# Second layer of a fused attention and feed-forward kernel by seven block products, in a phase of its own

## The chip, the cores and the metric

One core of one Trainium2 chip runs the whole program. The metric is the device time of one execution in microseconds (us); the figure before is the median of three runs. Engines are named as the profile names them: PE (matrix engine; PEld is its weight load), DVE (VectorE), ACT (ScalarE), POOL (GpSimd), SP (SyncE, which here only issues DMAs).

## The reference, cut to what matters

```python
kv  = einsum('bhsd,bhse->bhde', k, v)          # 8 batches, 8 heads, 576 positions, 64 wide
out = einsum('bhsd,bhde->bhse', q, kv)
x   = out / sqrt(mean(out * out, -1) + 1e-6) * g_norm      # to [4608 tokens, 512]
h   = x @ w_in                                  # 512 -> 2048
y   = gelu(h) @ w_out                           # 2048 -> 512, gelu with erf
```

All arrays are fp32.

## The kernel before, in words

The 4608 tokens are worked on in nine chunks (0 to 8) of 512. For a chunk, linear attention and its normalisation give `o` (four tiles of 128 features by 512 tokens), the first layer gives 16 tiles `h` of 128 by 512, GELU makes them into `g`, and the second layer adds 16 products into four PSUM banks `acc0` to `acc3`, one for 128 tokens. While one chunk is in the two layers, the attention of the next is prepared: `project` and `squares` (ACT squares and copies), `reduce`, `fold`, `rsqrt` (nine small DVE instructions), `scale` (a DVE transposition that spreads the factors, through the single buffer `sq`, and a multiplication). `sum_kv` and `split_kv` make the key-value matrices two chunks ahead.

PE multiplies in a fast form that keeps fewer mantissa bits than fp32. So each operand is split in two parts, a high one (a cast by ACT) and a low one (a subtraction by DVE or POOL, "low" below), and a product takes three matmuls: high by high, high by low, low by high. `split_q`, `high_block`/`low_block` and `gelu`/`rest` make such pairs.

From chunk 2 on (`PLAIN = 2`) the first layer multiplies 2 by 2 blocks with seven products instead of eight (Winograd's form of Strassen's scheme): pairs of h tiles, j = 0 to 7, in `layer1_pair`. Sums of weight blocks are made once, in chunk 1 (`combine`, `high_sums`, `low_sums`), and are written to DRAM as `products`; sums of activation blocks (T1 to T4, `add_blocks`) are made for each chunk. Per pair there are 7 x 6 matmuls of 256 columns (line 454); DVE adds the products up in PSUM (line 446). The products come back from DRAM through a ring of four tiles of 512 KB (`load_products`), a fetch being issued when the matmuls of the tile that it replaces are done. The second layer is plain: 16 x 12 matmuls of 512 columns per chunk (line 573), with `w_out`'s two parts lying in SBUF throughout. PE takes turns: a pair of the first layer, then the two second-layer products of the pair before.

The schedule is manual: on each engine the instructions stand in the order in which the code is written, and semaphores are put in from the data's dependencies. The DMAs stand in one queue, SP's, and one that waits holds those behind it.

Of the kernel before, what the change touches and what calls it, by code (L numbers as in the profile page):

```python
# [16 lines left out]
P = 128  # L17
# [5 lines left out]
PLAIN = 2  # L23
HALF = CH // 2
RING = 4
# [11 lines left out]
def linear_attn_rms_gelu_ffn(  # L37
# [31 lines left out]
    ps_acc = ctx.enter_context(tc.tile_pool(name="ps_acc", bufs=1, space=PSUM))  # L69
    ps_h = ctx.enter_context(tc.tile_pool(name="ps_h", bufs=2, space=PSUM))  # L70
    ps_a = ctx.enter_context(tc.tile_pool(name="ps_a", bufs=2, space=PSUM))
    dram = ctx.enter_context(tc.tile_pool(name="dram", bufs=1, space=bass.MemoryType.DRAM))

    HI, LO = slice(0, DM), slice(DM, 2 * DM)
    kv_h = [const.tile([P, NP, P], F32R, name=f"kv_h{s}") for s in range(2)]
# [7 lines left out]
    AWAY, ROOM = 48, 64  # L83

    def block_tile(name, dtype):
        ring = name in [f"w_in{i}" for i in range(RING)]
        return const.tile([P, 2 * DM + (ROOM if ring else 0)], dtype, name=name)
# [20 lines left out]
    def load_tails(b):  # L108

        tails = const.tile([P, 2 * DM], F32, name="w_in4")[:TAIL].rearrange("p (a n) -> p a n", a=NP)  # L110
        nc.sync.dma_start(out=tails[:, 2:], in_=kv_tail[b, :, 2:])
        for p in (2, 3):
            kv_in[b, p].append((tails[:, p, :P], tails[:, p, P:]))

    def load_kv(b, p):
# [4 lines left out]
        elif b == PLAIN + 1 and p > 1:  # L120
            main = const.tile([P, 2 * DM], F32, name=f"w_in{8 + p}")
# [26 lines left out]
    def sum_kv(b, pairs, ps=None):  # L148

        first = 0 if ps is not None else pairs[0]  # L150
        if ps is None:
            ps = kv_ps[b, first] = ps_a.tile([P, 512], F32, name="ps_a")
# [21 lines left out]
    class Attn:  # L174
# [34 lines left out]
        def project(self, p):  # L209
            qh, ql = self.qs.pop(p)  # L210
            ps = ps_a.tile([P, 512], F32, name="ps_a")
# [34 lines left out]
        def fold(self, n=NP):  # L246
            ps = ps_a.tile([P, 512], F32, name="ps_a")[:, :n * NB]
            nc.tensor.matmul(
                out=ps.rearrange("p (g b) -> p g b", g=n), lhsT=fold, rhs=self.part[:, :n, :],
# [35 lines left out]
        def scale(self, p):  # L285
# [3 lines left out]
            nc.vector.tensor_tensor(out=o, in0=o, in1=bc, op=ALU.mult)  # L289
# [27 lines left out]
        def add_blocks(self, k):  # L317
# [12 lines left out]
            nc.vector.tensor_tensor(out=t, in0=a, in1=b, op=op)  # L330
            self.sums[k] = t

        def high_block(self, n):

            x = piece_tile(self.c, n)
# [14 lines left out]
    NT2 = NPR * NF // 4  # L350
# [8 lines left out]
    def piece_tile(c, n):  # L359
        k = (["x2", "x3"] + [f"w_in{i}" for i in range(5, 10)],  # L360
             ["x0", "x1", "x4", "x5"] + [f"w_in{i}" for i in range(10, 13)])[c % 2][n]
        return const.tile([P, 2, 2, HALF], F32R, name=k)

    products = [dram.tile([P, 2 * DM], F32, name=f"products{t}") for t in range(NT2)]

    def product_out(j, k, src):

        n = NPR * j + k
        to = products[n // 2][:, n % 2 * DM:(n % 2 + 1) * DM]
        nc.sync.dma_start(out=to.rearrange("p (a n) -> p a n", a=2), in_=src.bitcast(F32))  # L370
# [3 lines left out]
    def combine(j, second):  # L374

        if not second:
            whole.clear()
            for a in range(2):
# [4 lines left out]
                if a == 0:  # L383
                    product_out(j, 0, t[:, :, :HALF])
                    product_out(j, 4, t[:, :, HALF:])
                else:
                    product_out(j, 3, t[:, :, HALF:])
# [24 lines left out]
    def low_sums():  # L412
        for (j, second), (s, t) in halved.items():
# [3 lines left out]
            for a, k in enumerate((6, 5) if second else (1, 2)):  # L417
                product_out(j, k, t[:, a])
        halved.clear()

    ring = {}

    def load_products(t):
        if t < (NCH - PLAIN) * NT2:
            reused(t % RING, F32R)
            to, src = kept[t % RING], products[t % NT2]
            first = [not n % NPR for n in (2 * t, 2 * t + 1)]
            for a in range(2):
                at = a * DM + (a * ROOM if first[a] else AWAY)
                ring[2 * t + a] = to[:, at:at + DM]  # L430
            if any(first):
# [632 lines left out]
```

## Time and profile before

| | |
|---|---|
| median of the runs | 823.49 us (822.92 to 824.34, three runs) |
| profiled execution: span from first to last instruction | 821.7 us; the profile gives no other time for it |
| PE, PEld busy | 816.0 us (99%), 721.8 us (88%) |
| DVE, ACT, POOL busy | 496.1 us (60%), 313.8 us (38%), 65.7 us (8%) |
| DMA | 174.99 MB, mean 213 GB/s |
| plain second layer, line 573 | 46% of the chain that ended last |
| first layer by blocks, line 454 | 33% of it |

The chain that ended last is followed back from the last instruction, at each step to what released it. PE is in it nearly all the time: what PE does, one thing after the other, is the kernel's time, and what the other engines do counts where PE waits for it.

### The profile page before, as it was taken

To read this page: it belongs to the slowest core of one execution; us is meant where nothing else is said; L and a number is where in the kernel's file an instruction comes from. 1 tells how busy PE (TensorE), PEld (TensorE's weight loads), DVE (VectorE), ACT (ScalarE), POOL (GpSimd) and SP (SyncE) were. 2 spreads that over 40 slices of the span, in tenths; PEclk is the share of its full clock that TensorE was granted. 3 is DMA by queue.
4 is the path that set the end of the run, shared out by engine and by line. 5 is a ranking of instruction groups with operands and counts; after the bars stand their busy time and mean duration, and the time that the engine had idled before them with its cause. 6 is when DMAs were issued, how large, how long until landed. Compare 5 with 4: busy or idle time off the path is not lost.

```text
span 821.7 us, 13904 instructions
## 1 busy us (share of the span) xinstructions
PE 816.0 (99%) x5390; PEld 721.8 (88%) x5390; DVE 496.1 (60%) x980; ACT 313.8 (38%) x578; POOL 65.7 (8%) x69
## 2 busy tenths in 40 slices
PE   9999999999999999999999999999999999999998
PEld 7688888887999999999989999999899999999997
DVE  3999847678446745575457554674477456754443
ACT  2788544344432343232432353143423442323221
POOL 1000020102010100010100101010001000100000
PEclk9999999999999999999999999999999999999999
DMA  9981337787594569556855678456555665556551
GB/s 348 406 346 52 116 99 259 244 270 262 166 354 146 179 226 351 160 179 202 310 197 179 206 248 296 150 179 225 197 180 181 205 231 175 183 168 243 177 171 52
DMA packets 69670, 174.99 MB, mean 213 GB/s; under 512 B 7396, under 2 KB 16356, under 8 KB 69604
## 3 DMA queue, kind: packets, MB, share of 16 engines
q1 hardware_dynamic: 69600, 174.09, 61.4%
q8 instruction: 43, 0.70, 0.3%
q14 instruction: 23, 0.19, 0.1%
q10 hardware_dynamic: 4, 0.00, 0.0%
HBM read 149.95 MB, written 24.12 MB: 212 GB/s over the span
## 4 chain that ended last, share of the span: by engine, by line
PE 94%; DMA 2%; DVE 2%; issue 1%; SPq 0%; ACT 0%; DVEq 0%; ACTq 0%
PE acc L573 46%; PE ps_h L454 33%; PE ps_h L547 8%; PE ps_a L218 3%; PE ps_a L158 2%; PE ps_h L539 1%; DMA w_in<-kv_tail 1%; DMA out<-z 1%; PE ps_h L658 1%; PE acc L692 0%; DMA q<-qT 0%; DVE w_in L414 0%; DVE w L398 0%; DMA products<-x 0%; DVE gl L565 0%
## 5 line engine op out<-in xcount | busy, mean ns | idle before, releaser
L573 PE MATMUL acc<-w_out,gh 128*128 128x512 f32 x700 | 217.0, 391 | 0.0
L454 PE MATMUL ps_h<-w_in,w_in 128*128 128x256 f32 x1392 | 166.9, 276 | 0.0
L454 PEld LDWEIGHTS ps_h<-w_in,w_in 128*128 128x128 f32 x1392 | 161.9, 188 | 0.0
L573 PE MATMUL acc<-w_out,w_in 128*128 128x512 f32 x672 | 159.6, 392 | 0.0
L573 PEld LDWEIGHTS acc<-w_out,gh 128*128 128x128 f32 x700 | 129.2, 188 | 25.4
L573 PEld LDWEIGHTS acc<-w_out,w_in 128*128 128x128 f32 x672 | 123.9, 188 | 24.8
L573 PE MATMUL acc<-w_out,gl 128*128 128x512 f32 x350 | 136.4, 390 | 0.1
L559 ACT ACTIVATE gh<-ps_h 128x512 fp32r<-128x512 f32 x88 | 52.6, 597 | 202.3 <-DVE ps_h L446 146.5
L454 PEld LDWEIGHTS ps_h<-x,w_in 128*128 128x128 f32 x960 | 119.0, 189 | 4.4
L454 PE MATMUL ps_h<-x,w_in 128*128 128x256 f32 x960 | 119.8, 278 | 0.0
L464 DVE COPY w_in<-ps_h 128x256 f32<-128x256 f32 x56 | 23.8, 425 | 130.6 <-PE ps_h L454 130.6
L559 ACT ACTIVATE w_in<-ps_h 128x512 fp32r<-128x512 f32 x56 | 33.5, 598 | 178.1 <-DVE ps_h L446 178.1
L446 DVE TENSOR_TENSOR ps_h<-ps_h,w_in 128x256 f32<-128x256 f32 x168 | 72.6, 432 | 43.5 <-PE ps_h L454 39.6
L446 DVE TENSOR_TENSOR w_in<-ps_h,w_in 128x256 f32<-128x256 f32 x168 | 71.3, 424 | 42.4 <-PE ps_h L454 40.5
L547 PE MATMUL ps_h<-x,w_in 128*128 128x512 f32 x360 | 86.8, 390 | 0.0
L560 ACT ACTIVATE ps_h<-ps_h 128x512 f32<-128x512 f32 x144 | 85.5, 594 | 0.0
L565 DVE TENSOR_TENSOR gl<-ps_h,gh 128x512 fp32r<-128x512 f32 x88 | 60.4, 687 | 41.5 <-ACT ps_h L560 37.3
L547 PEld LDWEIGHTS ps_h<-x,w_in 128*128 128x128 f32 x360 | 67.4, 188 | 13.9 <-POOL x L306 0.2
L573 PEld LDWEIGHTS acc<-w_out,gl 128*128 128x128 f32 x350 | 65.7, 188 | 14.5 <-DVE gl L565 0.5
L565 DVE TENSOR_TENSOR w_in<-ps_h,w_in 128x512 fp32r<-128x512 f32 x56 | 38.4, 687 | 17.0 <-ACT ps_h L560 17.0
L206 POOL TENSOR_TENSOR ql<-q,qh 128x512 fp32r<-128x512 f32 x16 | 21.3, 1329 | 211.1 <-ACT qh L205 153.2
L341 POOL TENSOR_TENSOR w_in<-o,w_in 128x512 fp32r<-128x512 f32 x13 | 16.9, 1322 | 204.0 <-ACT w_in L336 204.0
(153 smaller groups left out, 641.8 us busy)
## 6 DMA issues: line engine op xcount, KB each, us to landing
w_in<-products SPq DMA_DIRECT2D x140, 512.0 KB, 4.6
w_in<-products SPq DMA_DIRECT2D x112, 256.0 KB, 4.9
products<-w_in SPq DMA_DIRECT2D x40, 256.0 KB, 3.4
w_in<-w_in SPq DMA_DIRECT2D x16, 512.0 KB, 10.2
kv_main<-kv_main SPq DMA_DIRECT2D x16, 512.0 KB, 7.7
w_out<-w_out SPq DMA_DIRECT2D x16, 512.0 KB, 10.2
q<-qT SPq DMA_DIRECT2D x15, 512.0 KB, 5.9
out<-w SPq DMA_DIRECT2D x18, 256.0 KB, 2.1
```

The costliest lines, as they stand in the source:

```text
L158: nc.tensor.matmul(out=ps[r, n * D:(n + 1) * D], lhsT=k[:, r], rhs=v[:, r], start=(j == 0), stop=(j == NJ),)
L206: eng.tensor_tensor(out=ql, in0=q, in1=qh.bitcast(F32), op=ALU.subtract)
L218: nc.tensor.matmul(out=ps[:, a:e], lhsT=w, rhs=x[:, a:e], start=(m == 0), stop=(m == 2))
L341: eng.tensor_tensor(out=x[:, 1], in0=self.block(OPERANDS[n]), in1=x[:, 0].bitcast(F32), op=ALU.subtract,)
L446: add = lambda out, x, y: nc.vector.tensor_tensor(out=out, in0=x, in1=y, op=ALU.add)
L454: nc.tensor.matmul(out=out, lhsT=y, rhs=x[:, z, kb], start=first and kb + i == 0, stop=kb == 1 and i == 2, skip_group_check=True,)
L464: nc.vector.tensor_copy(out=p1, in_=a[:, left])
L547: nc.tensor.matmul(out=h, lhsT=parts["in", i][:, w][:, p * P:(p + 1) * P], rhs=at.x[p][:, x], start=(m + p == 0), stop=(m == 2 and p == NP ...
L559: nc.scalar.activation(out=gh, in_=h, func=AF.Gelu)
L560: nc.scalar.activation(out=h, in_=h, func=AF.Gelu)
L565: nc.vector.tensor_tensor(out=gl, in0=h, in1=gh.bitcast(F32), op=ALU.subtract)
L573: nc.tensor.matmul(out=ps, lhsT=x[:, ts], rhs=parts["out", i][:, w], start=(i == 0 and m == 0), stop=(m == 2 and (i == NF - 1 or (i, t) == ...
```

## The change

From chunk 3 on (`FAST = 3`) a chunk goes in two phases. In the first phase the pairs of the first layer follow each other without second-layer work between; a pair is cut into a first part (products 0 to 3) and a second part (products 4 to 6), and the second part of pair j stands behind the first part of pair j + 1. Attention work stands between the parts (`within_layer1`). GELU is applied once and its result kept in fp32 (`blocks`), not split at once.

In the second phase the second layer too goes by seven block products (`class Fast`): blocks of 256 tokens by 256 features, four groups n of four h tiles for each product k, in the order of `TICKS`. A tick (k, n) is 12 matmuls of 256 columns. `ready` makes the two parts of its activation operand (ACT cast, DVE low), four ticks ahead; `combine` makes the sums and differences of activation blocks in place, on POOL for product 6 and 2 in groups 0 to 2, else on DVE; `after` adds up products and stores. `within_layer2` prepares the next chunk's first-layer operands: T1 to T4 on POOL, lows in turn on DVE and POOL. The multiplication in `scale` moves to POOL too.

`w_out`'s block sums are made in chunk 2: `sum_out` on POOL, `split_out` on ACT and DVE, written out by DMAs on ACT's queue (`send`); blocks that need no sum are written in chunk 1 on SP's queue (`raw_out`). The ring grows to six tiles and is fed from one list of fetches (`queue`) for both layers; eleven of the tiles stay in SBUF (`RESIDENT`). PSUM banks get fixed names. In chunks 0 to 2 the order on PE is as before; the last chunk ends with the second phase instead of `finish`.

```diff
-RING = 4
+FAST = 3
+RING = (0, 1, 2, 3, 10, 11)
...
-        def scale(self, p):
+        def scale(self, p, eng=nc.vector):
             bc = work.tile([P, CH], F32, name="sq")
             self.spread(p, bc)
             o = self.o[p]
-            nc.vector.tensor_tensor(out=o, in0=o, in1=bc, op=ALU.mult)
+            eng.tensor_tensor(out=o, in0=o, in1=bc, op=ALU.mult)
...
+    ORDER = (0, 2, 4, 6, 1, 3, 5)
+    GROUPS = NF // 4
+    TICKS = [(0, 0), (0, 1), (0, 2), (2, 0), (2, 1), (0, 3), (2, 2), (2, 3)]
+    TICKS += [(k, n) for k in ORDER[2:] for n in range(GROUPS)]
...
+    def second_part(at, j, blocks):
+
+        a, b, u, v = pairs_open.pop(j)
+        product(at, j, 4, a[:, left])
+        product(at, j, 5, a[:, right])
+        add(a[:, right], a[:, right], u[:, right])
+        product(at, j, 6, b[:, right])
+        add(v[:, left], b[:, right], u[:, left])
+        add(b, b, v)
+        if j % 2 == 0:
+            blocks[j // 2] = [take() for _ in range(2)]
+        for (name, t), ps in zip(blocks[j // 2], (a, b)):
+            nc.scalar.activation(
+                out=grid(t)[:, :, j % 2], in_=ps.rearrange("p (a n) -> p a n", a=2), func=AF.Gelu
+            )
...
+        def ready(self, i):
+
+            if i >= len(self.ticks):
+                return
+            k, n = self.ticks[i]
+            op = self.ops[i] = take(F32R)
+            src = self.source(k, n)
+            hi, lo = (op[1].rearrange("p (z k n) -> p z k n", z=2, k=2)[:, z] for z in range(2))
+            nc.scalar.copy(out=hi, in_=src)
+            nc.vector.tensor_tensor(out=lo, in0=src, in1=hi.bitcast(F32), op=ALU.subtract)
...
+    def sum_out(j):
+
+        eng = nc.gpsimd
+        (name, whole), (of, s) = take(), take()
+        for n in range(2):
+            w = parts["out", 2 * j + n].bitcast(F32)
+            add(whole[:, n * DM:(n + 1) * DM], w[:, HI], w[:, LO], eng=eng)
...
+    def within_layer1(c, j):
...
+                nxt.project(j, bank("a0"))
+                nxt.squares(j)
+                if j < 2:
+                    nxt.split_q(2 + j)
+            if j == NP:
+                ps = bank("a0")
+                nxt.inv = nxt.rsqrt(nxt.fold(ps))
...
+            if j == 5:
+                sum_kv(c + 2, (2, 3), kv_ps[c + 2, 0])
+                split_kv(c + 2, range(NP))
+        if aft:
+            if j == 1:
+                aft.load(0)
+            if j in (4, 5):
+                aft.split_q(j - 4)
+        if nxt and j in (5, 6):
+            nxt.scale(2 * j - 9, nc.gpsimd)
...
+            if i == 0:
+                for k in ("T3", "T1", "T2", "T4"):
+                    attn[c + 1].add_blocks(k, nc.gpsimd)
+            if i % step == step - 1 and i // step < NPR:
+                n = i // step
+                next_piece(c, n, nc.gpsimd if n % 2 else nc.vector)
...
+    for c in range(FAST, NCH):
+        at = attn[c]
+        blocks = {}
+        layer = Fast(c, blocks)
+        for j, second in parts_of_layer1():
...
+            if (j, second) == (NJ2 - 1, False):
+                free.extend(names.pop((c, n)) for n in range(4))
+                for i in (3, 4):
+                    layer.ready(i)
+            if second and j % 2:
+                last = j == NJ2 - 1
+                layer.combine(6, j // 2, nc.vector if last else nc.gpsimd)
+                layer.ready(TICKS.index((0, j // 2)))
+                layer.combine(2, j // 2, nc.vector if last else nc.gpsimd)
+        free.extend(names.pop((c, n)) for n in range(4, NPR))
+        for i in range(len(layer.ticks)):
+            if i + layer.AHEAD > TICKS.index((0, GROUPS - 1)):
+                layer.ready(i + layer.AHEAD)
+            if 5 <= i < 5 + GROUPS:
+                layer.combine(3, i - 5)
+            if 9 <= i < 9 + GROUPS:
+                layer.combine(1, i - 9)
+            layer.matmuls(i)
+            layer.after(i)
+            within_layer2(c, layer, i)
```

How this moves instructions, at three places of chunk 5. Names are those of the tiles with the number of the buffer; numbers behind are partitions by elements. First PE, before: a pair of the first layer (line 454; `ps_h` is its PSUM bank, the second name is the ring's tile) and the first of the second-layer products behind it (line 573).

```order
L454 MATMUL ps_h<-x_7247,w_in_1483 128x256 x6
L454 MATMUL ps_h<-w_in_7249,w_in_1492 128x256 x6
L454 MATMUL ps_h<-w_in_7307,w_in_1492 128x256 x6
L454 MATMUL ps_h<-w_in_7212,w_in_2050 128x256 x6
L454 MATMUL ps_h<-w_in_7214,w_in_2050 128x256 x6
L454 MATMUL ps_h<-w_in_7210,w_in_2052 128x256 x6
L573 MATMUL acc_6773<-w_out_1138,gh 128x512 x2
L573 MATMUL acc_6773<-w_out_1138,gl 128x512
```

PE now, at the change of phase: the second parts of pairs 6 and 7 (line 523), then ticks 0 to 5 (line 1140).

```order
L523 MATMUL h_5980<-w_out_5327,w_in_2070 128x256 x6
L523 MATMUL h_5980<-w_out_5380,w_in_2070 128x256 x6
L523 MATMUL h_5981<-w_out_5437,x_3243 128x256 x6
L523 MATMUL acc_6075<-w_out_5327,w_in_2072 128x256 x6
L523 MATMUL acc_6075<-w_out_5380,w_in_2072 128x256 x6
L523 MATMUL acc_6076<-w_out_5437,x_3243 128x256 x6
L1140 MATMUL acc_6175<-w_in_2198,x_5727 128x256 x12
L1140 MATMUL acc_6175<-w_in_2200,w_out_5899 128x256 x12
L1140 MATMUL acc_6175<-w_in_1471,w_out_6071 128x256 x12
L1140 MATMUL acc_6233<-w_in_1480,w_out_6111 128x256 x12
L1140 MATMUL acc_6233<-w_in_2070,w_in_6114 128x256 x12
L1140 MATMUL acc_6175<-w_in_3402,w_out_6171 128x256 x12
```

The 512-column matmuls between the pairs are gone; the second layer's operands are needed only behind the last pair, and its weights now come through the ring (`w_in_2198`, `w_in_2200`, ...). Second, DVE, before: kv halves, scaling, one pair of the first layer and its lows (line 565).

```order
L170 TENSOR_TENSOR kv_l_77<-ps_a,kv_h_75 64x4x64 x2
L293 STREAM_TRANSPOSE sq<-y 128x512
L289 TENSOR_TENSOR o<-o,sq 128x512
L464 COPY w_in_2181<-ps_h 128x256
L446 TENSOR_TENSOR w_in_2181<-ps_h,w_in_2181 128x256 x2
L446 TENSOR_TENSOR ps_h<-ps_h,w_in_2181 128x256
L446 TENSOR_TENSOR w_in_2181<-ps_h,w_in_2181 128x256
L446 TENSOR_TENSOR ps_h<-ps_h,w_in_2181 128x256 x2
L565 TENSOR_TENSOR w_in_2234<-ps_h,w_in_2234 128x512
L565 TENSOR_TENSOR w_in_2238<-ps_h,w_in_2238 128x512
```

DVE now: the end of pair 6, the last spreading of factors, the end of pair 7, then combinations (line 1107), lows of ticks (line 1118) and a low for the next chunk (line 354).

```order
L514 TENSOR_TENSOR h_5981<-h_5981,gl 128x512
L307 STREAM_TRANSPOSE sq<-y 128x512
L514 TENSOR_TENSOR acc_6075<-acc_6075,gh 128x256
L514 TENSOR_TENSOR gl<-acc_6076,gh 128x256
L514 TENSOR_TENSOR acc_6076<-acc_6076,gl 128x512
L1107 TENSOR_TENSOR w_out_6139<-x_6140,w_out_6139 128x512
L1118 TENSOR_TENSOR w_out_6171<-w_out_6139,w_out_6171 128x512
L1107 TENSOR_TENSOR w_out_6139<-w_out_6139 128x512
L1118 TENSOR_TENSOR w_out_6209<-w_in_5958,w_out_6209 128x512
L354 TENSOR_TENSOR w_out_6227<-o,w_out_6227 128x512
L1118 TENSOR_TENSOR w_out_6230<-w_out_6139,w_out_6230 128x512
```

The multiplications of `scale` have left DVE, and behind the last pair stands a row of instructions that read and write SBUF only. Third, POOL, before: all that it has in a chunk, splits of q (line 206) and two lows (line 341).

```order
L206 TENSOR_TENSOR ql<-q,qh 128x512
L206 TENSOR_TENSOR w_in_5109<-q,w_in_5109 128x512
L206 TENSOR_TENSOR ql<-q,qh 128x512
L341 TENSOR_TENSOR w_in_5562<-o,w_in_5562 128x512
L341 TENSOR_TENSOR w_in_5564<-o,w_in_5564 128x512
L206 TENSOR_TENSOR w_in_5663<-q,w_in_5663 128x512
```

POOL now, from pair 4 to the start of the second phase: splits of q (line 217), scaling (line 303), combinations (line 1107), T3, T1, T2, T4 (line 344).

```order
L217 TENSOR_TENSOR ql<-q,qh 128x512
L303 TENSOR_TENSOR o<-o,sq 128x512
L217 TENSOR_TENSOR w_in_6064<-q,w_in_6064 128x512
L303 TENSOR_TENSOR o<-o,sq 128x512
L1107 TENSOR_TENSOR w_in_5958<-w_in_5959,w_in_5958 128x512
L1107 TENSOR_TENSOR w_in_5958<-w_in_5958 128x512
L303 TENSOR_TENSOR o<-o,sq 128x512 x2
L344 TENSOR_TENSOR z<-o 128x512
L344 TENSOR_TENSOR o<-o 128x2x256
L344 TENSOR_TENSOR w<-z,o 128x512
L344 TENSOR_TENSOR z<-o,w 128x512
```

Twelve instructions now stand behind each other on POOL where two splits and two lows stood, and DVE's queue at that place waits for POOL's multiplications through the buffer `sq`.

423 lines of the change are left out of this document (332 added, 91 removed).

## The prediction

> **What bounds the kernel now.** First the page: the engines, and the chain of work that ended last.
> ```profile
> span 821.7 us, 13904 instructions
> PE 816.0 (99%) x5390; PEld 721.8 (88%) x5390; DVE 496.1 (60%) x980; ACT 313.8 (38%) x578; POOL 65.7 (8%) x69
> PE 94%; DMA 2%; DVE 2%; issue 1%; SPq 0%; ACT 0%; DVEq 0%; ACTq 0%
> ```
> TensorE (PE) is busy 99% and is 94% of the chain. Next, that chain in order of time through chunk 3 (start, length, what).
> ```profile
> 295.66 4.79 PE ps_h L454 x42
> 300.45 0.68 PE ps_a L218 x6
> ...
> 333.98 0.17 PE ps_a L248 x2
> 334.15 2.48 PE ps_a L158 x80
> ...
> 342.30 4.80 PE ps_h L454 x42
> 347.09 5.46 PE acc L573 x24
> ...
> 383.34 4.79 PE ps_h L454 x42
> ```
> One chunk is 383.34 - 295.66 = 87.7 us and PE never waits in it: eight times a pair of the first layer (4.8) and two blocks of the second (5.46), and 5.6 of projections, key-value sums and fold. A matmul of 256 columns takes 4.795/42 = 0.1142 us, one of 512 takes 5.46/24 = 0.2275. Then the stretches (busy us of PE, PEld, DVE, ACT, POOL; clock; DMA share; GB/s): a saturated load at the start, chunk 1, and a steady piece.
> ```profile
> 30.00:40.00 10.00, 10.00 (x47) 8.38 (x47) 9.00 (x17) 8.86 (x17) 0.00 (x0) 1.00 1.02 408
> 100.00:190.00 90.00, 89.91 (x473) 74.39 (x472) 63.16 (x114) 37.20 (x72) 13.47 (x10) 1.00 0.61 209
> 370.00:460.00 90.00, 90.00 (x644) 81.78 (x643) 52.58 (x107) 31.57 (x59) 7.72 (x6) 1.00 0.66 222
> ```
> In the steady piece VectorE (DVE) has 37 of 90 us free, GpSimd (POOL) nearly all, and the DMA engines move 222 GB/s where they have moved 408. The clock is 1.00.
>
> **Term 1, PE: minus 31.9.** Per chunk the plain second layer is 8 x 5.46 = 43.7 us. The block form is 28 ticks (7 products x 4 groups) of 12 matmuls of 256 columns: 336 x 0.1142 = 38.4, one tick 1.37. No row has these operands. Half of a 512-column matmul would make it 38.2 and the L454 rows, same shape and same reloading of the stationary side, 38.4; I take L454. Six chunks (3 to 8) save 5.3 each: 31.9. That gives 821.7 - 31.9 = 789.8 us of span, if nothing else moves.
>
> **Term 2, who prepares the operands: plus 24.** A tick needs its activations split into a high half (ACT) and a low half (DVE); 28 lows replace 16, ten adds of 512 ("combinations") come to DVE and six to POOL, and POOL takes over the scaling, the sums T1 to T4 and three lows: 21 instructions of POOL per chunk, six before. In the second phase itself DVE has some 42 instructions of 0.61 against 38.4 us: it fits. The tight place is the end of the first phase, where the normalisation of the next chunk, the last pairs and the first operands of the second phase stand behind each other in DVE's queue. The costs are read from a stretch of chunk 2 (DVE in order of time: start, length, what, idle before).
> ```profile
> 242.94 0.42 DVE L464 COPY w_in<-ps_h 128x256 f32<-128x256 f32 x1 [3.81 <-PE ps_h L454]
> 243.40 0.42 DVE L446 TENSOR_TENSOR w_in<-ps_h,w_in 128x256 f32<-128x256 f32 x1
> ...
> 246.80 0.90 DVE L446 TENSOR_TENSOR ps_h<-ps_h,w_in 128x256 f32<-128x256 f32 x2
> 247.61 0.68 DVE L565 TENSOR_TENSOR gl<-ps_h,gh 128x512 fp32r<-128x512 f32 x1
> 248.85 0.69 DVE L565 TENSOR_TENSOR gl<-ps_h,gh 128x512 fp32r<-128x512 f32 x1 [0.56 <-ACT ps_h L560]
> 249.46 0.21 DVE L263 TENSOR_SCALAR m<-ps_a 128x64 f32<-128x64 f32 x1
> ...
> 251.64 0.41 DVE L170 TENSOR_TENSOR kv_l<-ps_a,kv_h 64x256 fp32r<-64x256 f32 x1
> 252.48 0.43 DVE L170 TENSOR_TENSOR kv_l<-ps_a,kv_h 64x256 fp32r<-64x256 f32 x1 [0.43 <-ACT kv_h L169]
> 252.94 0.71 DVE L293 STREAM_TRANSPOSE sq<-y 128x512 f32<-128x512 f32 x1
> 253.75 0.69 DVE L289 TENSOR_TENSOR o<-o,sq 128x512 f32<-128x512 f32 x1
> ```
> Starts tell the price in a queue: 0.46 for 256 columns with a dependency, 0.61 for 512 (248.85 to 249.46), 2.2 for the inverse root (to 251.64), 1.3 for the two kv halves with their hand-over to ACT, 0.73 for a transposition.
>
> Take chunks 3 to 5, from the end of PE's second part of pair 4 to the first matmul of tick 6 that reads a low half. PE has there: fold 0.17, first parts 6 and 7 (24 matmuls, 2.74 each), second parts 5, 6, 7 (18 matmuls, 2.06 each), half of the 2.48 of kv sums, six ticks 8.2, and 0.23: 21.5 us. DVE has: the tail of pair 4 1.1, inverse root 2.2, first parts 2 x 1.34, second parts 3 x 1.5, four transpositions 2.9, kv 1.3 and half a us until ACT comes to it, five lows and two combinations 4.3, the GELU's hand-over 0.55: 20.05. So 1.45 us is left, before any meeting with POOL. POOL runs eleven or twelve instructions of 1.29 in those 21 us, and this is what a meeting costs (first POOL, then DVE, chunk 1; then a pair of groups by shape, mean ns after the bar).
> ```profile
> 184.94 1.29 POOL L341 TENSOR_TENSOR x<-o,x 128x512 fp32r<-128x512 f32 x1 [28.38 <-PE acc L573]
> 186.19 1.47 POOL L206 TENSOR_TENSOR ql<-q,qh 128x512 fp32r<-128x512 f32 x1
> 184.99 1.52 DVE L398 TENSOR_TENSOR w<-z,w 128x256 f32<-128x256 f32 x1
> 186.43 1.78 DVE L414 TENSOR_TENSOR w_in<-w,w_in 128x512 fp32r<-128x512 f32 x1
> 219.39 1.29 POOL L206 TENSOR_TENSOR ql<-q,qh 128x512 fp32r<-128x512 f32 x1 [21.19 <-PE ps_h L454]
> 220.55 0.42 DVE L446 TENSOR_TENSOR w_in<-ps_h,w_in 128x256 f32<-128x256 f32 x1
> L341 DVE TENSOR_TENSOR x<-o,x 128x512 fp32r<-128x512 f32 x13 | 12.7, 974 | 0.0
> L341 DVE TENSOR_TENSOR w_in<-z,w_in 128x512 fp32r<-128x512 f32 x11 | 7.5, 686 | 0.5 <-ACT w_in L336 0.2
> ```
> With both inputs in SBUF, the DVE instruction under a POOL instruction took 1.78 instead of 0.68 and the small one 1.52 instead of 0.42: 1.1 us each, in turn with POOL. With one input in PSUM (220.55) it took its usual 0.42. The Trainium skill ("SBUF — State Buffer", section "Who interferes with whom") says that a DVE instruction with two SBUF inputs and a GpSimd one that reads SBUF lock each other out of a shared port, the loser fully blocked; the 1.78 agrees, and by that rule every meeting costs its full price, which is the second rival below.
>
> Eight such meetings are due in the stretch: the inverse root, the five lows, the two combinations (lines 1118 and 1107 of the changed kernel, opposite POOL's q split, scaling, combinations and T sums). A meeting costs between 0.3 (974 - 686 ns, the mean of a group that met POOL now and then) and 1.1. The early four fall at random within 1.29, half of it 0.65; the late ones stand face to face, nearer 1.1, unless POOL is through. I take 0.75. Stall before tick 6: 8 x 0.75 - 1.45 = 4.55. Up to tick 16 DVE has two instructions per tick (1.22 of 1.37), so it gains little, and two more of POOL's lows come: 0.8. Chunks 3 to 5: 5.3 each. Chunk 6 has no kv work (DVE 1.8 less, PE 1.24 less): 4.8. Chunk 7 has no q split either, six meetings: 6 x 0.75 - 2.0 + 0.8 = 3.3. Chunk 8 prepares nothing: 0. Sum 24. With 0.3 a meeting the same sum is 3.4, with 1.1 it is 40.8.
>
> **Term 3, chunk 2: plus 2.** Two lows more per pair on DVE (1.2 us) and 5.2 us of POOL (two sums of 512, four of 256) make w_out's sums. What DVE had to spare at the pairs' starts:
> ```profile
> 266.31 0.42 DVE L464 COPY w_in<-ps_h 128x256 f32<-128x256 f32 x1 [0.78 <-PE ps_h L454]
> 276.57 0.43 DVE L464 COPY w_in<-ps_h 128x256 f32<-128x256 f32 x1 [0.19 <-PE ps_h L454]
> ```
> Two of eight pairs run over, by 0.4 and 1.0, with some meetings more; 0 if the waits inside a pair absorb it, 4 if not.
>
> **Term 4, DMA and queues: 0.** A fast chunk fetches 45 tiles of 0.524 MB, with 4.7 MB of q, kv and output 28.3 MB: 343 GB/s over 82.4 us, under 408. Six tiles in the ring give a fetch five tiles' time, at least 6.9 us:
> ```profile
> w_in<-products SPq DMA_DIRECT2D x140, 512.0 KB, 4.6
> ```
> Against 4.6 from issue to landing some 2.5 us are to spare. On SP's queue the q load waits for POOL's split of the chunk before and holds the fetches behind it by about as much (0 to 0.5 per chunk). Chunk 1's 18 more DMAs hide under its DMA share of 0.61, the four per pair on ACT's queue under an ACT that is busy a third; if that cover is gone, kv tails or GELUs come late, 1 us at most. The end is as before, one add and one DMA.
>
> Sum: 789.8 + 24 + 2 = 815.8 of span. The median of the runs, 823.49, lies 1.8 above the profiled span, so 817.6.
>
> **Rivals.** (a) The lock is cheap, 0.3 a meeting, and DVE keeps pace: for it the mean of 974; against it that POOL's work quadruples. 789.8 + 3.4 + 0 to 2 + 1.8 = 795 to 797. (b) Slower than before: every meeting at its full price, in this one place, between first and second phase. The sum grows by 47 us per us of price (40.8 - 3.4 over 0.8); the saving is gone at 0.88, and at 1.1 it is 789.8 + 40.8 + 4 + 1.8 = 836. For it 186.43, where two queues stood face to face; against it that POOL must have an instruction ready each time. (c) The fetches become the bound, against the 408. The second phase alone moves 21 tiles, q, kv and output, 13.9 MB in 38.4 us, 362 GB/s; were only 323 to be had, the chunk would be 87.7 as before and the change worth nothing from this alone: 823. The Trainium skill ("DMA: Bandwidth & Descriptors", section "Specifications") gives about 358 GB/s per core for HBM; by that the second phase would last 38.8, 0.4 more per chunk, 820 in all; the trace's 408 speaks against it.
>
> **Chances.** Forecast (price 0.6 to 0.84): 0.40, 810 to 822. (a), below 0.6: 0.25. (b), above 0.88: 0.27. (c): 0.08. About 0.2% (1.6 us) can be told from no change. Faster: the forecast nearly whole, (a), a little of (c): 0.62. Same 0.10, slower 0.28. The likeliest one's range is 810 to 822; for 8 in 10 both rivals are cut half through: 797 to 831.
>
> **What would show it.** PE busy about 783 with 25 us of idle, nearly all in chunks 3 to 7 around the change of phase, released by DVE lows of line 1118; none in chunk 8, whose 28 ticks take 38.4. DVE's two-SBUF instructions mean 0.8 to 1.0 us there, the 512-column add on PSUM (line 514) 0.69. Wrong in the steps: ticks longer than 1.37 (term 1); PE waiting for the ring's DMAs (term 4); stalls without any POOL beside them (term 2's count of DVE's work).

## The result and the profile after

The changed kernel takes 843.88 us (842.56 to 846.76), the kernel before, on the same chip, 823.54: ratio 1.0255, 95% interval 1.0235 to 1.0274. Forecast were 817.6 and a range of 797 to 831. First the page of the profiled execution.

```profile
span 841.8 us, 16154 instructions
PE 807.5 (96%) x6248; PEld 751.7 (89%) x6248; DVE 613.7 (73%) x1063; ACT 354.9 (42%) x654; POOL 267.8 (32%) x198
PE 74%; DVE 18%; DMA 4%; ACT 2%; issue 1%; POOL 0%; SPq 0%; ACTq 0%; DVEq 0%
```

PE was busy 816.0 us before and is busy 807.5 now: 8.5 less, where 33 less were forecast (783). Span less busy time is 34.3 us, 28.6 more than before, where 26 more were forecast. So most of the miss is on the busy side; 6.5 of it is waiting all the same, because PE counts as busy while a stopped stream drains and refills (by the starts below, its waits grew by 35.1 us, its idle time by 28.6). Next, who ended PE's waits (engine, line, waited for: us, times, longest).

```profile
PE acc L1140 <- DVE w_out L1118: 12.8, 9, 1.7
PE h L523 <- DVE w_in L514: 7.0, 5, 3.0
PE acc L523 <- DVE gl L514: 4.0, 4, 1.3
PE acc L682 <- DVE gl L674: 1.8, 1, 1.8
PE acc L523 <- DMA w_in<-products_in: 1.1, 1, 1.1
```

The first row and the third are the change of phase, as forecast; the second is chunk 2. The chain that ended last shows one change of phase, in chunk 4 (start, length, what).

```profile
437.54 0.44 DVE gl L514
...
451.14 2.76 DVE w_out L1118 x2
...
457.95 1.26 DVE w_out L1107
459.21 1.70 DVE w_out L1118
460.93 1.66 DVE w_out L1107
462.58 1.68 DVE w_out L1118
464.31 14.08 PE acc L1140 x118
478.39 5.65 PE a L1140 x48
```

From 437.5 to 464.3 DVE carries the chain, with 1.9 us of ACT in it, then PE. How long the matmuls take where PE waits for nobody is to be read in chunk 8, in the same chain:

```profile
774.52 4.93 PE acc L523 x42
...
798.42 22.64 PE acc L1140 x192
821.06 5.62 PE a L1140 x48
```

No stall, but four ticks take 5.62 us, 1.405 each, where 1.37 was forecast, and 42 matmuls of the first layer, which keeps its products, take 4.93, where 42 took 4.79 before. The granted clock is 1.00 in both profiles. Matmuls of one shape have become slower.

To put a figure on that I took, from the traces, the distance from each matmul's start to the next one's. Undisturbed it is 0.1133 us for 256 columns and 0.2268 for 512. What a distance has above that counts as "rate", or as "waits" if the distance is more than about 13% over. Sums in us, without the 24 matmuls of 512 columns in the first 28 us, which are alike in all:

```
kernel                  first layer   ticks   512 columns   waits
                        (rate)        (rate)  (rate)
before                      2.0         -         1.7         2.5
after                       9.5        8.4        3.0        37.6
e1_before_pad48             8.6         -         3.5         2.5
e2_pad64                    6.5       10.0        0.4        39.3
e3_pad64_offset48           6.3        3.5        0.5        43.2
e4_sums_on_vector           6.5        3.6        0.6        48.9
e5_before_no_zero          10.5         -         1.1         3.0
e6_zero_back                6.8        3.7        0.6        43.0
e7_prepare_late             7.2        4.5        0.6        57.3
e8_chunk2_q_later           6.4        3.5        0.5        38.8
e9_before_all16            10.6         -         1.7         2.2
e10_prepare_early           6.8        3.4        0.5        16.4
e11_in_offset16             7.3        3.4        0.6        37.3
e12_early_and_offset16      8.5        3.4        0.5        17.2
```

Not all of the last column is waiting for an operand. The granted clock is 1.00 throughout in most of these profiles, but in six it falls to 0.50 behind a stall, for 3.4 us at a time: once in e2, e7 and e12, twice in e6 and e10, five times in e4. Each time costs some 1.7 us, most of which is counted in the column: 8.5 in e4.

The change takes 6 x (192 x 0.2268 - 336 x 0.1133) = 32.9 us of PE work away, its rates give 17.1 back (20.9 against 3.8 with small rests) and its waits 35.1: +19.3, against 20.1 between the spans.

### The profile page after: what moved, and what is told of

Its sections match the earlier page's. It is cut to its first block, busy times and chain, and to the rows that moved or that the text cites. A ratio compares the mean times of both kernels' runs of the same rounds, so it can differ in the third digit from the quotient of the medians.

```text
span 841.8 us, 16154 instructions
## 1 busy us (share of the span) xinstructions
PE 807.5 (96%) x6248; PEld 751.7 (89%) x6248; DVE 613.7 (73%) x1063; ACT 354.9 (42%) x654; POOL 267.8 (32%) x198
## 4 chain that ended last, share of the span: by engine, by line
PE 74%; DVE 18%; DMA 4%; ACT 2%; issue 1%; POOL 0%; SPq 0%; ACTq 0%; DVEq 0%
PE acc L1140 15%; PE acc L523 13%; PE acc L682 12%; PE h L523 11%; PE h L655 10%; PE a L1140 8%; DVE w_out L1118 4%; PE a L230 3%; DMA w_in<-products_in 2%; DVE acc L514 2%; DVE sq L307 2%; DVE w_out L1107 1%; PE a L169 1%; DVE gl L514 1%; DMA kv_main<-kv_main 1%
## 5 line engine op out<-in xcount | busy, mean ns | idle before, releaser
L1140 PE MATMUL acc<-w_in,w_out 128*128 128x256 f32 x900 | 114.0, 281 | 12.8 <-DVE w_out L1118 12.8
L523 PE MATMUL acc<-w_out,w_in 128*128 128x256 f32 x930 | 119.5, 281 | 3.0 <-DVE gl L514 2.8
L1140 PEld LDWEIGHTS acc<-w_in,w_out 128*128 128x128 f32 x900 | 108.9, 189 | 14.7 <-DVE w_out L1118 14.7
L682 PE MATMUL acc<-w_out,gh 128*128 128x512 f32 x312 | 97.5, 394 | 0.0
L655 PE MATMUL h<-x,w_in 128*128 128x512 f32 x360 | 87.9, 393 | 0.0
L655 PEld LDWEIGHTS h<-x,w_in 128*128 128x128 f32 x360 | 67.5, 188 | 14.9
L523 PE MATMUL h<-w_out,w_in 128*128 128x256 f32 x558 | 71.9, 281 | 0.0
L682 PEld LDWEIGHTS acc<-w_out,gh 128*128 128x128 f32 x312 | 58.0, 188 | 12.3
L523 PEld LDWEIGHTS h<-w_out,w_in 128*128 128x128 f32 x558 | 68.2, 188 | 0.1
L682 PE MATMUL acc<-w_out,gl 128*128 128x512 f32 x156 | 61.3, 393 | 1.8 <-DVE gl L674 1.8
```

The costliest lines, as they stand in the source:

```text
L523: nc.tensor.matmul(out=out, lhsT=y, rhs=x[:, z, kb], start=first and kb + i == 0, stop=kb == 1 and i == 2, skip_group_check=True,)
L655: nc.tensor.matmul(out=h, lhsT=parts["in", i][:, w][:, p * P:(p + 1) * P], rhs=at.x[p][:, x], start=(m + p == 0), stop=(m == 2 and p == NP ...
L682: nc.tensor.matmul(out=ps, lhsT=x[:, ts], rhs=parts["out", i][:, w], start=(i == 0 and m == 0), stop=(m == 2 and (i == NF - 1 or (i, t) == ...
L1140: nc.tensor.matmul(out=ps[:, a * HALF:(a + 1) * HALF], lhsT=x[:, at], rhs=y, start=(k in (0, 2, 1) and n + p + a + m == 0), stop=(n == GRO ...
```

## Experiments

Each is timed against the kernel before on the same chip; e1 to e4, e5 to e8 and e9 to e12 are on three chips, where the kernel before takes 823.1, 823.5 and 823.2. e1, e5 and e9 are made from the kernel before, the others from the changed kernel: e4 and e6 to e8 build on e3, e10 to e12 on e8. Five questions: why the matmuls are slower, what the stalls are made of, what chunk 2 waits for, whether the stalls can be moved, and whether the slow rate can be avoided.

### Addresses: the pads alone, in the kernel before

The change made the ring tiles 48 elements longer than a block (64 before), and six of them for four. In the built program every tile of weights, blocks, activations or GELU stood at 192 modulo 256 bytes before; now the tiles between and behind the ring's stand at 0, 64, 128 or 192.

```diff
-    AWAY, ROOM = 48, 64
+    AWAY, ROOM = 48, 48
```

> The kernel before with one number changed: the four ring tiles are 48 elements longer than a block and no longer 64, so every tile behind them starts 192 bytes further on, modulo 256, instead of 0. Nothing else moves. Theory A, TensorE's rate follows the SBUF addresses of the two operands: from starts of consecutive matmuls in both profiles, grouped by both addresses modulo 256, a 256-column matmul takes 0.114 us in some groups and 0.119 in others, one of 512 columns 0.228 against 0.232; with this kernel's addresses the sum over its matmuls grows by 9.6 us, to about 833. Theory B, the slower matmuls of the changed kernel come from its DMA traffic or from the other engines: no change, 823.5.

831.46 us against 823.12, ratio 1.0101 (1.0086 to 1.0116). The page says where (span, engines):

```profile
span 829.9 us, 13904 instructions
PE 824.4 (99%) x5390; PEld 728.7 (88%) x5390; DVE 496.2 (60%) x980; ACT 314.2 (38%) x578; POOL 65.7 (8%) x69
```

and the chain shows a pair of the first layer, 4.79 before:

```profile
297.34 4.91 PE ps_h L454 x42
```

PE is busy 8.4 us more with the same instructions, no wait more, the same DMA bytes and the same work on the other engines. Theory A holds, and B falls as the only cause: addresses alone cost 8 us. The edit does a little more than shift tiles: in half of the pairs `ROOM` also sets where product 0 lies in its tile, and what that place is worth is the question of e5. So the 8 us are the price of addresses, not of the shift of the tiles by itself.

### The changed kernel with its tiles back in line

```diff
-        return const.tile([P, 2 * DM + (AWAY if ring else 0)], dtype, name=name)
+        return const.tile([P, 2 * DM + (64 if ring else 0)], dtype, name=name)
...
-            away = AWAY if key[0] == "in" else AWAY // 3
+            away = AWAY
```

The first edit alone is e2, both are e3. For room, both also give up the second buffer of a scratch tile of the inverse root.

> The changed kernel with ring tiles 64 elements longer than a block (48 before), so that all tiles start at the same address modulo 256 as in the kernel before; one scratch tile of the inverse root loses its second buffer to make room. Operands of the second layer then stand at 0 (moving) and 192 (stationary) modulo 256, a pair that neither profile has. Theory A: first layer and plain chunks gain; with that unknown pair fast (0.114) the sum over the matmuls falls by 13 us, with it slow (0.119) by 5: 831 to 839. Theory B: 844.

> As e2_pad64, and the second layer's operands also sit 48 elements into their ring tile (16 before): moving 128, stationary 192 modulo 256, a pair that took 0.114 us in the changed kernel. Theory A: the sum over the matmuls falls by 12.9 us against the changed kernel; since TensorE then needs the operands earlier, the stalls at the change of phase grow by 2 to 4: 832 to 834. Theory B: 844.

e2: 844.92, ratio 1.0263 (1.0242 to 1.0283): no gain, outside what I expected, and Theory B's number. The trace parts the two. The first layer and the plain chunks did win 5.6 us of rate, as A has it, and the unknown pair (moving 0, stationary 192) is a slow one: the ticks go from 8.4 to 10.0 us above the undisturbed rate, which with 1.7 us of half clock eats 3.3 of the 5.6. e3: 839.12, ratio 1.0187 (1.0159 to 1.0215), 4.8 us less than the changed kernel where 10 to 12 were expected. The rates give 10.5 (20.9 to 10.4), near the 12.9; but waits grow by 5.6, more than my 2 to 4. In chunks 4 to 7 they grow by 1.8 (19.6 to 21.4): a faster PE arrives earlier at operands that come no earlier. Another 3.7 is chunk 3, where PE now waits up to 2.1 us for a fetch and 1.9 for ACT in front of a projection; why there is not shown. From e2 to e3 nothing moves but the ticks' weight operands, by 128 bytes, and the ticks win 6.5 us. In the chain of e3:

```profile
400.12 5.52 PE a L1140 x48
405.64 2.72 PE h L523 x24
...
419.66 2.85 PE h L523 x24
```

The second and the third row are 24 matmuls of one form, the first parts of two pairs, at the same addresses modulo 256 and 14 us apart: 0.1133 and 0.1188 each. So the addresses are not all; what ran before matters too, and for long. By single starts between 405 and 432 us, distances are 113, 113, 114 ns up to a product from a resident tile (both operands at 192, 119 to 121 ns) and the projection behind it, and then 118, 118, 117 through everything that follows, until a stall.

### The product that brings the short distances back

In the kernel before, product 0 of each pair, and it alone, is read from an offset at which both operands stand at 192; it takes 0.119. In e5 it loses that place:

```diff
-                at = a * DM + (a * ROOM if first[a] else AWAY)
+                at = a * DM + AWAY
```

> The kernel before, with the operand of each pair's product 0 put 48 elements into its ring tile like the six others (before: at 0 or 64 elements, where both operands of the matmul start at 192 modulo 256). Theory P, the rate has a memory: in e3_pad64_offset48 matmuls with one and the same pair of addresses (192, 128) take 0.1133 us in some stretches and 0.1177 in others; a slow stretch begins behind a projection, key-value sums, a fold or a stall, and a fast one behind products with both operands at 192. Without those, the slow state stays after the first disturbance: 2352 x 0.0044 less the 2.0 us above 0.1133 that these products cost now, up to 8 us slower, 827 to 831. Theory Q, each pair of addresses has its own price and no memory: 2 us faster, 821.

830.66 against 823.49, ratio 1.0091 (1.0075 to 1.0106): Theory P. In the chain all 42 matmuls are slow, and the 512-column ones beside them are not:

```profile
296.98 4.95 PE ps_h L454 x42
...
302.63 5.45 PE acc L573 x24
```

4.95 / 42 = 0.1179, in every pair of the steady chunks. A product that is itself 5% slower keeps 36 others fast, and leaving it out costs 7 us. The changed kernel's `fetch` has no such place for product 0.

```diff
+            if key[0] == "in" and key[2] == 0:
+                t = ring[n] = [kept[i][:, a * (DM + 64):][:, :DM] for a in range(2)]
+                t[1] = kept[i][:, DM + away:2 * DM + away]
...
```

> As e3_pad64_offset48, and product 0 of each pair reads its weights from the start of the ring tile (two transfers of half a tile, as in the kernel before), so that both operands start at 192 modulo 256. Theory P: the first layer returns to 0.1133 behind each product 0; of its 6.3 us above that rate some 3.5 stay: 836. Theory Q: 336 matmuls become 0.0057 slower, 841.

840.18, ratio 1.0206 (1.0190 to 1.0222): not told from e3, and nearer to Theory Q's 841 than to P's 836; but 3.4 us of it are half clock, which e3's profile doesn't have, so the time does not decide. The rates do, against P: 6.8 us for 6.3, where P leaves 3.5 and Q makes 8.2 of it. The edit does not bring the short distances back here. Behind a projection (L230) the pair runs on slowly, product 0 at 117 to 119 ns and the others at 117 to 118:

```profile
418.45 0.76 PE a L230 x6
419.21 2.85 PE h L532 x24
```

In the kernel before product 0 follows matmuls of 512 columns with both operands at 192; in this stretch it follows a projection of 320 and 192 columns. What I made of it, that a product at equal places shortens the distances whatever came before, is refuted.

A last try at a rule: in e3's ticks (moving 128, stationary 192) the rate came back by itself within three matmuls of every disturbance. Perhaps moving 64 bytes below stationary is safe. First on e5, then on e8 (below):

```diff
-    AWAY, ROOM = 48, 64
+    AWAY, ROOM = 16, 64
```

> As e5_before_no_zero (the kernel before, all seven blocks at one offset in the ring tile), with offset 16 for 48: moving operand at 192, stationary at 0 modulo 256, that is the moving one 64 bytes below the stationary one. In the second layer of e3 the pair (128, 192), with the same difference, came back to 0.1133 us within three matmuls of every disturbance; (192, 128), with the opposite one, did not. Theory R, a matmul whose moving operand stands 64 bytes below the stationary one modulo 256 is fast whatever came before: the 10.5 us above 0.1133 of e5 fall to near 0, 821. Rival, only the product with both operands at the same place brings the fast state back: as e5, about 830.

```diff
-            away = AWAY
+            away = AWAY // 3 if key[0] == "in" else AWAY
```

> As e8_chunk2_q_later, with the first layer's operands 16 elements into the ring tile for 48: moving 192, stationary 0 modulo 256. Theory R: of the first layer's 6.4 us above 0.1133 only the 1.6 us of product 6 from resident tiles (both at 192) stay: 4.8 less, 831. Rival, as in the kernel before offsets make no difference behind a disturbance: 835.

831.66 (1.0085 to 1.0119) and 837.65 (1.0142 to 1.0195, against 835.45 for e8, from which it differs by this offset alone): Theory R falls twice. (192, 0) runs at 118 ns as (192, 128) does in e5. What sets and keeps the longer distances stays open; shown are their price (0.0044 us per matmul of 256 columns), that they depend on the two operands' addresses and on what ran before, and that they can last for tens of us.

### The stalls: GpSimd's meetings with VectorE

In chunk 4 of the changed kernel, first VectorE, then GpSimd, each in order of time (start, length, engine, line, out<-in):

```profile
452.12 1.78 DVE L1118 TENSOR_TENSOR w_out<-w_in,w_out 128x512 fp32r<-128x512 f32 x1
...
459.13 1.76 DVE L1118 TENSOR_TENSOR w_out<-w_out,w_out 128x512 fp32r<-128x512 f32 x1
460.93 1.66 DVE L1107 TENSOR_TENSOR w_out<-w_out 128x512 f32<-128x512 f32 x1
462.51 1.75 DVE L1118 TENSOR_TENSOR w_out<-w_in,w_out 128x512 fp32r<-128x512 f32 x1
...
465.38 0.68 DVE L1118 TENSOR_TENSOR w_in<-w_in,w_in 128x512 fp32r<-128x512 f32 x1
```

```profile
458.74 1.60 POOL L344 TENSOR_TENSOR o<-o 128x512 f32<-128x512 f32 x1
460.31 1.73 POOL L344 TENSOR_TENSOR w<-z,o 128x512 f32<-128x512 f32 x1
462.11 1.60 POOL L344 TENSOR_TENSOR z<-o,w 128x512 f32<-128x512 f32 x1
```

Beside GpSimd's sums the lows take 1.7 us, behind them 0.68. Eight VectorE instructions of this stretch lost 6.9 us that way, 0.87 each. In e4 the scalings and sums T1 to T4 are VectorE's own.

```diff
-                    attn[c + 1].add_blocks(k, nc.gpsimd)
+                    attn[c + 1].add_blocks(k)
...
-            nxt.scale(2 * j - 9, nc.gpsimd)
+            nxt.scale(2 * j - 9)
...
```

> As e3_pad64_offset48, and eight instructions per chunk (four scalings, the sums T1 to T4) go from GpSimd back to VectorE. Theory A with the lock: in chunk 4 of the changed kernel the eight VectorE instructions with two SBUF inputs that met GpSimd took 6.9 us more than alone; these meetings mostly vanish, VectorE gets 8 x 0.61 = 4.9 us of work: 0 to 2 us less per chunk, 824 to 834. Rival, VectorE is simply full there and the meetings cost nothing: 4.9 us more in each of five chunks, about 858.

846.05, ratio 1.0284 (1.0255 to 1.0313): 6.9 us above e3, between the theories' times. By the trace of chunk 4: VectorE's stretch from the tail of pair 4 to the first low of tick 6 went from 26.3 (438.00 to 464.26, changed kernel) to 27.6. Three meetings were left (1.20 for 0.23, 1.33 and 1.74 for 0.68: 2.7 us), so 4.2 were saved, and 4.9 were added. "Mostly vanish" was too much; the price of a meeting holds. Giving an instruction from GpSimd back to VectorE is nearly a wash there: it costs 0.61 and saves some 0.53. The 6.9 us of the whole kernel are another matter: its profile has 17 us at half clock, 8.5 us lost, e3's none, and the mean clock is 0.985 to 0.990 in its four runs, 0.997 to 1.000 in e3's. Taken off, they leave e4 no slower than e3, so the time decides between the theories no more than it did, and what is left is the trace of chunk 4.

### Chunk 2

There GpSimd's sums of w_out ran into the inverse root. Its split of q, one pair later, holds them back:

```diff
-            if at in ((3, 0), (7, 0)):
+            if at in ((4, 0), (7, 0)):
```

> As e3_pad64_offset48, with chunk 2's split of q for chunk 4 one pair later, which holds GpSimd's sums of w_out (they stand behind it in the queue) back from the pair in which VectorE computes the inverse root. There five small VectorE instructions took 0.67 to 1.03 instead of 0.23 us and one lower half 1.78 instead of 0.68. Lock: the stall of 3.6 us in that pair goes, 836. Rival, VectorE is late in chunk 2 by its count of instructions: 839.

835.45, ratio 1.0158 (1.0129 to 1.0186), 3.7 us below e3, where the lock has 3 and the rival none. The two intervals overlap, so the trace has to carry it: the same instructions, in the changed kernel and in e8, where GpSimd has nothing to do at that time:

```profile
255.55 1.78 DVE L1200 TENSOR_TENSOR x<-x,x 128x512 fp32r<-128x512 f32 x1
...
257.50 1.03 DVE L280 TENSOR_SCALAR y<-m 128x64 int32<-128x64 int32 x1
258.57 0.81 DVE L286 SCALAR_TENSOR_TENSOR t<-y 128x64 f32<-128x64 f32 x1
```

```profile
254.76 0.68 DVE L1200 TENSOR_TENSOR x<-x,x 128x512 fp32r<-128x512 f32 x1
...
255.61 0.20 DVE L280 TENSOR_SCALAR y<-m 128x64 int32<-128x64 int32 x1
255.84 0.23 DVE L286 SCALAR_TENSOR_TENSOR t<-y 128x64 f32<-128x64 f32 x1
```

So the lock is shown. What it was worth is less than the medians say: by the starts, chunk 2 waits 6.0 us for e3's 8.5. The stall of 3.7 in that pair is gone, but PE waits 2.6 for 1.0 in the next pair. The trace also has 1.6 less in chunk 3, and that this comes of the edit is not shown.

### Moving the preparation: later, then earlier

e7 takes the next chunk's inverse root, scalings, sums and operands out of the first phase and puts them into ticks 11 to 23.

```diff
+            if i == 11:
+                nxt.inv = nxt.rsqrt(nxt.fold(bank("a1")))
+            if 12 <= i < 12 + NP:
+                nxt.scale(i - 12, nc.gpsimd)
+            if i == 16:
+                for k in ("T3", "T1", "T2", "T4"):
+                    nxt.add_blocks(k, nc.gpsimd)
...
```

> As e3_pad64_offset48, but the next chunk's inverse root, scalings, sums T1 to T4 and operands are made in ticks 11 to 23 of the second phase and no longer around the change of phase. If the stalls there (4.1 + 4.2 + 4.6 + 3.4 us of idle in chunks 4 to 7 of that kernel, 3.4 in chunk 3) come from VectorE's queue with its GpSimd meetings, they vanish: 818 to 824. Rival: VectorE's 9 us without work at the end of the second phase are not enough, and as much waiting comes back in the ticks behind the twelfth: 836 to 842.

854.64, ratio 1.0348 (1.0295 to 1.0400), 15.5 above e3. The stall at the change of phase did go; the meetings came along, and the ticks' lows, four ahead of PE, could not pay for them (VectorE, then GpSimd):

```profile
489.81 1.77 DVE L354 TENSOR_TENSOR w_out<-o,w_out 128x512 fp32r<-128x512 f32 x1
491.50 1.75 DVE L1118 TENSOR_TENSOR w_out<-w_out,w_out 128x512 fp32r<-128x512 f32 x1
```

```profile
489.41 1.61 POOL L344 TENSOR_TENSOR z<-o 128x512 f32<-128x512 f32 x1
491.11 1.59 POOL L344 TENSOR_TENSOR o<-o 128x512 f32<-128x512 f32 x1
```

That is outside both ranges: the rival named the place, but I had not priced the meetings there. Fetches too make PE wait in e7, 0.5 to 2.1 us at a time at the start of the first phase, which the changed kernel has in chunk 3 alone.

e10 goes the other way: two projections in each of the first two parts, fold and inverse root in the third, scalings and sums before pair 5.

```diff
-            if j < NP:
-                nxt.project(j, bank("a0"))
-                nxt.squares(j)
...
+            if j < 2:
+                for p in (2 * j, 2 * j + 1):
+                    nxt.project(p, bank(f"a{p % 2}"))
+                    nxt.squares(p)
...
-            if j == NP:
+            if j == 2:
                 ps = bank("a0")
                 nxt.inv = nxt.rsqrt(nxt.fold(ps))
...
-        if nxt and j in (5, 6):
-            nxt.scale(2 * j - 9, nc.gpsimd)
+        if nxt and j in (3, 4):
+            nxt.scale(2 * j - 5, nc.gpsimd)
+        if nxt and j == 4:
+            for k in ("T3", "T1", "T2", "T4"):
+                nxt.add_blocks(k, nc.gpsimd)
...
```

> As e8_chunk2_q_later, but in chunks 3 to 7 the next chunk's projections go two at a time in the first two parts, and its inverse root, scalings and sums T1 to T4 two parts earlier, where VectorE was busy 5.5 of 10 us. If the stalls at the change of phase come from VectorE's queue with its GpSimd meetings (idle 3.4 + 4.1 + 4.2 + 4.5 + 3.4 us in chunks 3 to 7 there), they vanish without coming back in the second phase, since that gets no new work: 815 to 820. Rival: the same stalls appear in the middle of the first phase: 832 to 838.

> e10_prepare_early and e11_in_offset16 together: 835.5 - 18 - 4.8 = 811 to 816 if both theories hold; 826 to 831 if only the second does.

e10: 812.74 us, ratio 0.9877 (0.9862 to 0.9892), faster than both kernels and 2.3 better than my range. The range counted the stalls as idle time of the page, 19.6 us; by starts the waits in chunks 3 to 7 fall by 25.7 (29.8 in e8, 4.1 here). e12: 814.22 (0.9881 to 0.9910). That lies in the range for both theories, but by e10's step alone: the offset again gives nothing. The page of e10, its chain across the change of phase of chunk 4, and VectorE there, one after the other:

```profile
span 810.5 us, 16146 instructions
PE 797.4 (98%) x6248; PEld 745.9 (92%) x6248; DVE 586.8 (72%) x1063; ACT 355.5 (44%) x654; POOL 256.1 (32%) x198
```

```profile
438.56 2.12 PE h L523 x18
440.68 2.29 PE acc L523 x18
442.96 22.08 PE acc L1140 x192
```

```profile
440.76 1.80 DVE L1118 TENSOR_TENSOR w_out<-x,w_out 128x512 fp32r<-128x512 f32 x1
442.49 1.78 DVE L1118 TENSOR_TENSOR w_out<-w_in,w_out 128x512 fp32r<-128x512 f32 x1
```

PE goes through without a gap: 192 matmuls of the ticks in 22.08, 0.1150 each. Meetings are still there (1.80, 1.78), but VectorE now has room for them, and PE does not wait. Waits fall from 38.8 us in e8 to 16.4, those in the ticks from 18.1 to 0. What is left lies before chunk 3 for the most part, and some 3 us of that are half clock.

## Why the prediction was wrong, step by step

**Term 1 (forecast -31.9, measured -15.8) is the step that failed.** The count of matmuls was right: 32.9 us by undisturbed rates. "Same shape and same reloading of the stationary side" was taken as enough for the same 0.1142 us; the change also moved every tile in SBUF, and shape does not fix the rate. It gave back 8.4 us in the ticks, 7.5 in the first layer, which the sum left as it was, and 1.2 in the plain chunks. e1 shows 8 us of this kind from addresses alone, e2 to e3 6.5 us from one operand's offset, e5 7 from the lost product 0. The text named the sign ("ticks longer than 1.37") and chunk 8 shows it, 1.405.

**Term 2 (forecast 24, measured 23.6) was right**, in its place and, part by part, nearly in its sizes: waits in chunks 3 to 7, by starts, are 5.0 (without 1.4 for fetches), 5.1, 5.3, 5.4 and 3.8, 1.1 of which the same chunks waited before; forecast 5.3, 5.3, 5.3, 4.8, 3.3. Eight meetings were counted and eight are there in chunk 4, at 0.87 for 0.75; VectorE's own work was 26.3 - 6.9 = 19.4 for 20.05. That the total comes so near is in part luck: the price was 1.0 too low over eight meetings, VectorE's work 0.65 too high, and the waits were measured against a PE that was slower than forecast (in e3, with less of term 1's loss, chunks 4 to 7 wait 21.4 for 19.6). Chunk 8 has none. As idle time of the page these waits are smaller (17.9), since PE counts as busy while a stopped stream drains and refills. Two things in the working are thin. First, the row at 220.55, an instruction with an input in PSUM, overlaps POOL's by 0.13 us only; the changed kernel's trace bears the reading out (line 514 at 449.76, inside a POOL instruction from 448.66 to 450.39, takes 0.42). Second, how the 0.8 of the second phase goes with the price isn't said: kept as it is, the sums at 0.3 and 1.1 a meeting are 7.1 and 37.5, where 3.4 and 40.8 stand. The outcome does not hang on it.

**Term 3 (forecast 2, measured 8.4)**: the "meetings more" in chunk 2 were not priced. Two adds and four sums per pair on GpSimd stand opposite the small instructions of the inverse root, five of which lost 2.9 us in one pair. e8 takes 2.5 us of chunk 2's waits back; the 6.0 that stay are not taken apart.

**Term 4 (forecast 0, measured 3.1)**: 1.4 in chunk 3 behind fetches and 1.7 in chunk 1. There three of the added DMAs stand in SP's queue ahead of the stores, VectorE waits 6.1 us for a store (4.2 before), and PE 1.9 for VectorE; small, and not tested. The DMA engines were not the bound: chunks 4 to 8 have no such wait, so rival (c) has no share. One slice of the page, in chunk 3, moves 398 GB/s, above the 358 that the Trainium skill ("DMA: Bandwidth & Descriptors", section "Specifications") gives for HBM.

**Rivals.** The time, 843.9, lies above rival (b)'s 836, but not for (b)'s reason: the meetings cost 0.87, not 1.1, just under the break-even of 0.88. The forecast gain was 5.9: term 1's miss alone turns the sign, and so would those of terms 3 and 4 together.

The sum of the misses: 16.1 (term 1) - 0.4 + 6.4 + 3.1, with 1.1 unassigned, makes the 26.3 us between forecast and result.

## What to carry to other kernels

When a change adds or resizes an SBUF tile, compare the time of matmuls it does not touch before explaining anything else: here a pad of 48 elements for 64 cost 8 us, and one operand's offset 6.5. Where a stall comes from an engine's queue, count its meetings with its neighbour at the measured price, and look for the stretch of the period where that engine has room; that was earlier, not later, and with the tiles back in line and chunk 2's sums held back it turned 2.5% slower into 1.2% faster. A step that makes PE faster first makes the stalls longer (1.8 us in chunks 4 to 7 of e3), so the two have to be judged together.

## What the runs showed of the hardware that was not expected

The rate of a stream of matmuls depends on where its two operands stand and has a memory: 0.1133, 0.118 or 0.120 us for the same shape, with the clock at 1.00. The Trainium skill ("TensorE: Matmul & The Clock Gate", section "Step-by-step: what each phase is for") says that loading the next weights doesn't steal SBUF read bandwidth from the running matmul. By that the weights' place should not count; here it does, by up to 6% (0.1133 to 0.120), and the measurement decides, though that the two reads meet in SBUF is not shown.

The clock can fall behind a stall. In e4 it was 0.50 for 3.4 us behind waits of PE of 2.9 to 3.9 us, in e10 behind waits of 2.2 and 2.6. But e3 has a wait of 3.7 and the changed kernel one of 3.2 without it, so what decides is not shown. A stall can then cost 1.7 us more than its length, and kernels with stalls are compared at their clocks first.

GpSimd can lose for long. One of its subtractions took 7.50 us where its like takes 1.29, while VectorE ran 0.68 us instructions with two SBUF inputs one after the other; the same one in the other four chunks took as long (7.56 us in the mean). It ended 1.24 us after VectorE began an instruction with one input in PSUM (GpSimd, then three of VectorE's):

```profile
474.08 7.50 POOL L354 TENSOR_TENSOR w_out<-z,w_out 128x512 fp32r<-128x512 f32 x1 [6.86 <-ACT w_out L349]
```

```profile
474.31 0.68 DVE L1118 TENSOR_TENSOR w_out<-w_in,w_out 128x512 fp32r<-128x512 f32 x1
474.92 0.68 DVE L1107 TENSOR_TENSOR w_in<-w_out,w_in 128x512 f32<-128x512 f32 x1
...
480.34 0.68 DVE L514 TENSOR_TENSOR gh<-acc,gh 128x512 f32<-128x512 f32 x1
```

The Trainium skill ("SBUF — State Buffer", section "Who interferes with whom") has the engine that issues first hold the shared pair for the whole instruction. That agrees with single meetings; that ten VectorE instructions in a row pass a waiting GpSimd one is more than it states.
